# Tap order of a convolution, placement of the first chunks' TensorE work, and order of the loads, in a fused convolution and gated MLP kernel

## Chip, cores, metric

One Trainium2 chip, one core. The metric is device time in microseconds (us). The kernel before took 718.42 us (median of 3 runs, 718.25 to 720.43). "TensorE", "VectorE", "ScalarE", "GpSimd" and "SyncE" are PE, DVE, ACT, POOL and SP in the profile's lines. SBUF and PSUM are the two memories in which the kernel puts its tiles; the matmuls write to PSUM, and to "evict" is to copy a result from there to SBUF. A "tap" is one of the filter's 7 weights, and here also the one VectorE instruction that applies it to one group of channels of one chunk. The "granted clock" is the share of TensorE's full clock that the profile shows, 1.00 at full.

## The reference

```python
# x: (8, 4096, 192); weight: (8 heads, 7 taps); w_in: (192, 2048); w_out: (2048, 192); beta: (2048,)
w = softmax(weight, axis=-1)                      # causal depthwise convolution, one filter per head
x_pad = concatenate([zeros(B, 6, D), x], axis=1)
conv[b, s, h, g] = sum_k w[h, k] * x_pad[b, s + k, h, g]        # 8 heads x 24 channels = 192
h = conv.reshape(B * S, D) @ w_in
g = h * sigmoid(beta * h)
out = g @ w_out
```

## The kernel before

The work goes in steps of 512 tokens of two batch halves (chunk 0 is split in two half steps of 256 tokens, so step 0 and 1 are chunk 0, and step s from 2 on is chunk s-1). The 192 channels lie as three groups of 64; the two halves of the batch fill the 128 partitions. In step s, piece u (16 of them) TensorE makes one hidden block of step s and the share u of the outputs of step s-1. VectorE, meanwhile, convolves the chunk of step s+2, tap by tap, and evicts outputs from PSUM. Chunks from 2 on reach SBUF by a cast to bf16 in DRAM (GpSimd queue) and a transposing DMA (SyncE queue). Chunk 0 and 1 are transposed by TensorE, and chunk 0 is also convolved by TensorE, with diagonal matrices, so that there is something to do early.

The taps, group by group; each of the last six reads what the one before wrote:

```python
    if k == 0:
        nc.vector.tensor_scalar_mul(dst, src, scalar)                          # L330
    else:
        nc.vector.scalar_tensor_tensor(                                        # L332
            out=dst, in0=src, scalar=scalar, in1=dst, op0=ALU.mult, op1=ALU.add)
return [lambda j=j, k=k: tap(j, k) for j in range(NG) for k in range(K)]
```

The eviction of outputs, in VectorE's same queue, which runs in program order (the timeline below shows an eviction wanted from about 45 us on run at 52.82, behind taps written ahead of it; `psum_o` has two buffers, so the outputs two allocations later wait for it):

```python
    nc.vector.tensor_copy(dst, po[:, 0, 0 : 2 * D])                            # L389
    nc.vector.tensor_tensor(dst, po[:, 1, 0 : 2 * D], dst, ALU.add)            # L390
```

The order of work in the first step, and the loop:

```python
extra = {(0, 1): first_xt,                  # TensorE transposes, second half of chunk 0
         (0, 3): lambda: copy_w_in(2),      # VectorE copies of w_in to the other 64 partitions
         (0, 4): first_conv,                # 21 diagonal matmuls, second half of chunk 0
         (0, 6): lambda: copy_w_in(3),
         (0, 8): second_xt}                 # 24 transposes: chunk 1, whose taps can start after this
for s in range(N_ST + 1):
    if s + 2 < N_ST:
        queue.extend(conv_ops(s + 2))
    for u in range(NF):
        if s < N_ST: hidden(s, u)
        if s > 0:    output(s - 1, u)
        if (s, u) in extra: extra[s, u]()
        if s > 0 or u > 8:
            for _ in range(4 if s == 0 else 2 - u % 2):
                if queue: queue.popleft()()
        # [cut] cast(s + 4) at u == 0, transposing DMA of chunk s + 2 at u == 1
```

Ahead of the loop GpSimd scales `w_out` by 1/beta (`prep_w_out`, four instructions) and then issues the casts of chunks 2 and 3.

Of the kernel before, what the change touches and what calls it, by code (L numbers as in the profile page):

```python
# [9 lines left out]
FP32 = mybir.dt.float32  # L10
FP32R = mybir.dt.float32r
BF16 = mybir.dt.bfloat16
# [5 lines left out]
def kernel(  # L18
# [17 lines left out]
    nc = tc.nc  # L36

    B, S, D = x.shape
    H, K = weight.shape
    F = moe_w_in.shape[1]  # L40
    group = D // H
    DG = 64
    NG = D // DG
    TOK = 512
    NF = F // 128
    PAD = K - 1
    HALO = 16
    BLK = 128
# [4 lines left out]
    steps = [(0, 0, TOK // 2), (0, TOK // 2, TOK // 2)]  # L53
# [6 lines left out]
    consts = ctx.enter_context(tc.tile_pool(name="consts", bufs=1))  # L60
    setup = ctx.enter_context(tc.tile_pool(name="setup", bufs=1))
# [4 lines left out]
    ct_pool = ctx.enter_context(tc.tile_pool(name="ct", bufs=3))  # L66
    g_pool = ctx.enter_context(tc.tile_pool(name="g", bufs=2))
    osb_pool = ctx.enter_context(tc.tile_pool(name="osb", bufs=3))
    psum_h = ctx.enter_context(
        tc.tile_pool(name="psum_h", bufs=2, space=bass.MemoryType.PSUM)  # L70
    )
    psum_o = ctx.enter_context(
        tc.tile_pool(name="psum_o", bufs=2, space=bass.MemoryType.PSUM)
    )
# [34 lines left out]
    NB = TOK // BLK  # L109
    HB = NB // 2  # L110
    x0 = setup.tile([128, NB, 2, D], FP32)
    x0b = setup.tile([128, NB, 2, D], BF16)
    x1b = setup.tile([128, NB, 2, D], BF16)

    def load_x(eng, dst, t0, b0, nb):
        for h in range(2):
            eng.dma_start(
                out=dst[:, b0 : b0 + nb, h, :],
                in_=x_v[0, t0 : t0 + nb * BLK, h, :].rearrange(
                    "(b q) d -> q b d", q=BLK  # L120
                ),
            )
# [1 line left out]
    cw8 = setup.tile([H, K], FP32)  # L124
    nc.scalar.dma_start(out=cw8, in_=weight)
    load_x(nc.sync, x0, 0, 0, HB)
    beta_q = setup.tile([NF, 128], FP32)
    nc.sync.dma_start(out=beta_q, in_=moe_beta.rearrange("(c p) -> c p", p=128))
    load_x(nc.sync, x0, HB * BLK, HB, HB)

    zeros = setup.tile([128, TOK], BF16)
# [10 lines left out]
    def load_w_in(i):  # L142
        cols = slice(i * FW, (i + 1) * FW)
        nc.gpsimd.dma_start(  # L144
            out=w_in_s[0:DG, :, cols],
            in_=moe_w_in[:, cols].rearrange("(c d) f -> d c f", c=NG),
        )

    def copy_w_in(i):
        cols = slice(i * FW, (i + 1) * FW)  # L150
        nc.vector.tensor_copy(w_in_s[DG : 2 * DG, :, cols], w_in_s[0:DG, :, cols])  # L151
# [9 lines left out]
        out=sel,  # L161
        in_=sel,
        compare_op=ALU.is_ge,
        fill=0.0,
# [5 lines left out]
        out=sel,  # L170
        in_=sel,
        compare_op=ALU.is_ge,
        fill=0.0,
# [3 lines left out]
    )  # L177
    ident = setup.tile([128, 128], FP32)
    make_identity(nc, ident)
    for i in range(1, NW):  # L180
        load_w_in(i)
    load_x(nc.gpsimd, x1b, TOK, 0, NB)
    w_out_raw = setup.tile([128, NF, D], FP32)
    w_out_v = moe_w_out.rearrange("(c p) d -> p c d", p=128)
    for c in range(0, NF, 4):
        nc.sync.dma_start(out=w_out_raw[:, c : c + 4, :], in_=w_out_v[:, c : c + 4, :])


    nmax = setup.tile([H, 1], FP32)
    nc.vector.reduce_max(nmax, cw8, axis=mybir.AxisListType.X, negate=True)  # L190
    ssum = setup.tile([H, 1], FP32)
    nc.scalar.activation(cw8, cw8, AF.Exp, bias=nmax, accum_out=ssum)
    nc.scalar.activation(warm, warm, AF.Silu)
    rsum = setup.tile([H, 1], FP32)
    nc.vector.reciprocal(rsum, ssum)
    nc.vector.tensor_scalar_mul(cw8, cw8, rsum)
    pc = psum_o.tile([128, 2, TOK], FP32, name="po")

    def fill(n):
        for _ in range(n):  # L200
            nc.tensor.matmul(pc[:, 1, :], zeros[:, 0:128], zeros, start=True, stop=True)  # L201

    fill(5)
    for c in range(NG):
# [4 lines left out]
            start=True,  # L209
            stop=True,  # L210
        )
    nc.tensor.transpose(pc[:, 0, 32 : 32 + NF], beta_q, ident[0:NF, 0:NF])
    fill(3)
    ident_b = setup.tile([128, 128], BF16)
    nc.vector.tensor_copy(ident_b, ident)
    nc.vector.tensor_copy(x0b[:, 0:HB], x0[:, 0:HB])
    cw = consts.tile([128, NG, K], FP32)
    nc.vector.tensor_copy(cw.rearrange("p c k -> p (c k)"), pc[:, 0, 0 : NG * K])
    beta = consts.tile([128, NF], FP32)
    nc.vector.tensor_copy(beta, pc[:, 0, 32 : 32 + NF])  # L220
    beta_r = setup.tile([128, NF], FP32)
    nc.vector.reciprocal(beta_r, beta)


    diag = setup.tile([128, NG, K, 128], FP32R)

    def diag_v(c):
        nc.vector.tensor_tensor(  # L228
            diag[:, c, :, :],
            ident.unsqueeze(1).to_broadcast((128, K, 128)),  # L230
            cw[:, c, :].unsqueeze(2).to_broadcast((128, K, 128)),
            ALU.mult,
        )

    def transposes(xb, b0, nb):
        pt = psum_o.tile([128, NG, nb * BLK], BF16, name="po")
        for b in range(nb):
            for c in range(NG):
                for h in range(2):
                    nc.tensor.transpose(  # L240
                        pt[h * DG : (h + 1) * DG, c, b * BLK : (b + 1) * BLK],
                        xb[:, b0 + b, h, c * DG : (c + 1) * DG],
                        ident_b,
                    )
        return pt

    xt0 = setup.tile([128, NG, HALO + TOK], FP32R)
    nc.vector.memset(xt0[:, :, 0:HALO].bitcast(FP32), 0.0)
    cts = {}

    def diag_conv(s, c, pv):
        n = steps[s][2]
        o = HALO - PAD + steps[s][1]
        for k in range(K):
            nc.tensor.matmul(  # L255
                pv[:, c, :],
                diag[:, c, k, :],
                xt0[:, c, o + k : o + k + n],
                start=(k == 0),
                stop=(k == K - 1),  # L260
            )

    n0 = HB * BLK
    pt = transposes(x0b, 0, HB)
    for k in range(K):
        nc.scalar.mul(diag[:, 0, k, :], ident, cw[:, 0, k : k + 1])  # L266
    diag_v(1)
    nc.scalar.copy(xt0[:, 0:2, HALO : HALO + n0], pt[:, 0:2, :])  # L268
    nc.vector.tensor_copy(xt0[:, 2, HALO : HALO + n0], pt[:, 2, :])
    diag_v(2)  # L270
    copy_w_in(0)
    ct = ct_pool.tile([128, NG, TOK], BF16, name="ct")
    cts[0] = ct
    pv = psum_h.tile([128, 4, n0], FP32, name="ph")
    for c in (1, 0, 2):
        diag_conv(0, c, pv)
        if c == 0:
            nc.scalar.copy(ct[:, c, 0:n0], pv[:, c, :])  # L278
        else:
            nc.vector.tensor_copy(ct[:, c, 0:n0], pv[:, c, :])  # L280
    nc.vector.tensor_copy(x0b[:, HB:NB], x0[:, HB:NB])
    copy_w_in(1)

    def first_xt():

        pt = transposes(x0b, HB, HB)
        nc.vector.tensor_copy(xt0[:, :, HALO + n0 :], pt)

    def first_conv():
        ct = ct_pool.tile([128, NG, TOK], BF16, name="ct")  # L290
        cts[1] = ct
        pv = psum_o.tile([128, 4, n0], FP32, name="po")
        for c in range(NG):
            diag_conv(1, c, pv)
        nc.vector.tensor_copy(ct[:, :, 0:n0], pv[:, 0:NG, :])  # L295

    def second_xt():
        xt = new_xt(1)
        pt = transposes(x1b, 0, NB)
        nc.vector.tensor_copy(xt[:, :, HALO - PAD : HALO], xt0[:, :, HALO + TOK - PAD :])  # L300
        nc.vector.tensor_copy(xt[:, :, HALO:], pt)

    w_out_s = consts.tile([128, NF, D], BF16)

# [14 lines left out]
    def conv_ops(s):  # L319
        ch, t0, n = steps[s]  # L320

        def tap(j, k):
            if j == k == 0:
                cts[s] = ct_pool.tile([128, NG, TOK], BF16, name="ct")
            o = HALO - PAD + k + t0
            src = xts[ch][:, j, o : o + n]
            dst = cts[s][:, j, 0:n]
            scalar = cw[:, j, k : k + 1]
# [4 lines that stand above are left out]
                    out=dst, in0=src, scalar=scalar, in1=dst, op0=ALU.mult, op1=ALU.add  # L333
                )

        return [lambda j=j, k=k: tap(j, k) for j in range(NG) for k in range(K)]

    gs = {}

# [22 lines left out]
    def output(s, u):  # L362
# [33 lines left out]
                )  # L396


    extra = {
        (0, 1): first_xt,  # L400
        (0, 3): lambda: copy_w_in(2),
        (0, 4): first_conv,
        (0, 6): lambda: copy_w_in(3),
        (0, 8): second_xt,
    }
    queue = deque()
    for s in range(N_ST + 1):
        if s + 2 < N_ST:
            queue.extend(conv_ops(s + 2))
        for u in range(NF):  # L410
            if s < N_ST:
                hidden(s, u)
            if s > 0:
                output(s - 1, u)
            if (s, u) in extra:
                extra[s, u]()
            if s > 0 or u > 8:
                for _ in range(4 if s == 0 else 2 - u % 2):
                    if queue:
                        queue.popleft()()  # L420
            if u == 0 and s + 4 < N_CH:
                cast(s + 4)
            if u == 1 and s + 2 < N_CH:
                xpose(s + 2)
# [30 lines left out]
```

## Time and profile before

| | before |
|---|---|
| time, median of 3 | 718.42 us |
| span of the profiled run | 717.5 us |
| TensorE / VectorE / ScalarE busy | 692.2 / 592.2 / 578.5 us |
| one piece (hidden and outputs) in the steady part | 1.308 us, 20.9 us per step |

TensorE is busy nearly all the span. These are the page's lines of busy time and one of its costliest groups, that of the taps (columns of a group: count, then busy time and mean ns of one, then idle time before them):

```profile
span 717.5 us, 24845 instructions
PE 692.2 (96%) x11465; PEld 529.2 (74%) x11465; DVE 592.2 (83%) x935; ACT 578.5 (81%) x543; POOL 67.3 (9%) x79
...
L332 DVE SCALAR_TENSOR_TENSOR ct<-xt,cw,ct 128x512 bf16<-128x512 bf16 x558 | 418.6, 750 | 16.6
```

From 100 to 600 us TensorE is busy 100.00 us in each 100 us, and VectorE 88.1 to 90.4 us, so nothing that VectorE does can matter there: a step costs VectorE less than TensorE's 20.9 us. Only the first 80 us have room. First the table of waits for 30 to 90 us (engine and line that waited, releaser: us in total, times, longest):

```profile
PE po L380 <- DVE osb L390: 10.7, 2, 8.3
```

Those two waits in the timeline of TensorE (start, length, what, count; in brackets the idle time before it and what ended it):

```profile
44.56 1.18 PE L349 MATMUL ph<-ct,w_in_s 64*128 64x512 bf16 x6
54.02 0.82 PE L380 MATMUL po<-w_out_s,g 64*128 64x192 bf16 x8 [8.28 <-DVE osb L390]
...
76.36 0.83 PE L349 MATMUL ph<-ct,w_in_s 64*128 64x512 bf16 x6
79.62 0.83 PE L380 MATMUL po<-w_out_s,g 64*128 64x192 bf16 x16 [2.43 <-DVE osb L390]
```

And why VectorE was late, in its own timeline:

```profile
30.24 0.35 DVE L330 TENSOR_SCALAR ct<-xt,cw 128x512 bf16<-128x512 bf16 x1
30.63 4.69 DVE L332 SCALAR_TENSOR_TENSOR ct<-xt,cw,ct 128x512 bf16<-128x512 bf16 x6
35.23 0.35 DVE L330 TENSOR_SCALAR ct<-xt,cw 128x512 bf16<-128x512 bf16 x1
...
52.82 0.55 DVE L389 COPY osb<-po 128x384 f32<-128x384 f32 x1
53.41 0.56 DVE L390 TENSOR_TENSOR osb<-po,osb 128x384 f32<-128x384 f32 x1
53.88 2.31 DVE L332 SCALAR_TENSOR_TENSOR ct<-xt,cw,ct 128x512 bf16<-128x512 bf16 x3
```

VectorE waits for nothing from 30.24 on. The eviction that TensorE needs from about 45 us on stands behind 32 taps. Two things can be read from the gaps between starts. Six dependent taps take 4.69 us, so they start (4.69 - 0.75) / 5 = 0.788 us apart. The next tap that depends on nothing starts at 35.23, before the end of the record in front of it (30.63 + 4.69 = 35.32): it overlaps by 0.09 us.

Last, the clock. The table of stretches (columns: busy time of each engine with counts, then the granted TensorE clock, DMA share, GB/s) shows that TensorE works at half clock for 3.5 us after the long wait:

```profile
50.70:54.00 3.30, 0.00 (x0) 0.00 (x0) 3.19 (x6) 0.00 (x0) 2.58 (x3) 0.50 2.44 156
54.00:57.50 3.50, 3.48 (x28) 2.21 (x29) 3.40 (x5) 1.11 (x1) 2.30 (x4) 0.52 2.45 156
57.50:60.00 2.50, 2.50 (x42) 1.70 (x38) 2.37 (x4) 2.20 (x3) 1.45 (x2) 1.00 2.05 189
```

### The profile page before, as it was taken

To read this page: it belongs to the slowest core of one execution; us is meant where nothing else is said; L and a number is where in the kernel's file an instruction comes from. 1 tells how busy PE (TensorE), PEld (TensorE's weight loads), DVE (VectorE), ACT (ScalarE), POOL (GpSimd) and SP (SyncE) were. 2 spreads that over 40 slices of the span, in tenths; PEclk is the share of its full clock that TensorE was granted. 3 is DMA by queue.
4 is the path that set the end of the run, shared out by engine and by line. 5 is a ranking of instruction groups with operands and counts; after the bars stand their busy time and mean duration, and the time that the engine had idled before them with its cause. 6 is when DMAs were issued, how large, how long until landed. Compare 5 with 4: busy or idle time off the path is not lost.

```text
span 717.5 us, 24845 instructions
## 1 busy us (share of the span) xinstructions
PE 692.2 (96%) x11465; PEld 529.2 (74%) x11465; DVE 592.2 (83%) x935; ACT 578.5 (81%) x543; POOL 67.3 (9%) x79
## 2 busy tenths in 40 slices
PE   6959899999999999999999999999999999999996
PEld 3646677777777777777777777777777777777776
DVE  3699999898988889898888989888898988887213
ACT  3658788888888888888888888888888888888881
POOL 6765551000000000000000000000000000000000
PEclk9999999999999999999999999999999999999999
DMA  9999999311223221132233112232211322211012
GB/s 198 125 157 166 166 170 172 68 49 44 68 68 52 64 70 49 43 69 68 52 64 69 49 44 68 68 53 62 69 51 42 70 68 53 62 46 46 25 46 68
DMA packets 183113, 54.57 MB, mean 76 GB/s; under 512 B 146384, under 2 KB 183008, under 8 KB 183008
## 3 DMA queue, kind: packets, MB, share of 16 engines
q0 software_dynamic: 97600, 13.31, 27.7%
q1 hardware_dynamic: 85392, 39.67, 23.5%
q8 instruction: 89, 1.46, 0.8%
q14 instruction: 16, 0.13, 0.1%
q10 hardware_dynamic: 16, 0.00, 0.0%
HBM read 28.98 MB, written 37.29 MB: 92 GB/s over the span
## 4 chain that ended last, share of the span: by engine, by line
PE 90%; DVE 7%; ACT 1%; DMA 1%; issue 0%; SPq 0%; DVEq 0%
PE po L380 45%; PE ph L349 43%; DVE ct L332 5%; DMA beta_q<-in_moe_beta_dram 1%; PE ph L255 1%; DVE ct L330 0%; DVE osb L390 0%; PE po L255 0%; DVE osb L389 0%; ACT diag L266 0%; ACT g L356 0%; DVE w_in_s L151 0%; PE po L240 0%; PE po L201 0%; DVE diag L228 0%
## 5 line engine op out<-in xcount | busy, mean ns | idle before, releaser
L356 ACT ACTIVATE g<-ph,beta 128x1024 bf16<-128x1024 f32 (+1 forms) x528 | 572.2, 1088 | 112.9 <-PE ph L349 108.8
L380 PEld LDWEIGHTS <-g 64*128 64x128 bf16 x8192 | 369.9, 94 | 113.8 <-issue 12.5
L380 PE MATMUL po<-w_out_s,g 64*128 64x192 bf16 x8192 | 430.9, 243 | 11.0 <-DVE osb L390 10.7
L332 DVE SCALAR_TENSOR_TENSOR ct<-xt,cw,ct 128x512 bf16<-128x512 bf16 x558 | 418.6, 750 | 16.6
L349 PE MATMUL ph<-ct,w_in_s 64*128 64x512 bf16 (+1 forms) x3168 | 428.7, 372 | 1.9 <-ACT g L356 1.3
L349 PEld LDWEIGHTS <-w_in_s 64*128 64x128 bf16 x3168 | 164.1, 94 | 57.2 <-issue 5.2
L389 DVE COPY osb<-po 128x384 f32<-128x384 f32 x128 | 71.4, 558 | 83.4 <-PE po L380 82.9
L390 DVE TENSOR_TENSOR osb<-po,osb 128x384 f32<-128x384 f32 x128 | 71.3, 557 | 4.4
L95 POOL DMA_DIRECT2D xd<-in_x_dram x60 | 54.9, 918 | 38.0 <-DMA xd<-in_x_dram 35.9
L330 DVE TENSOR_SCALAR ct<-xt,cw 128x512 bf16<-128x512 bf16 x93 | 32.9, 354 | 0.0
L255 PE MATMUL ph<-xt_151,diag 128*128 128x256 f32 x21 | 5.6, 439 | 4.6 <-ACT xt_151 L268 2.2
L255 PEld LDWEIGHTS ph<-xt_151,diag 128*128 128x128 f32 x21 | 4.7, 326 | 5.4 <-ACT xt_151 L268 2.4
L306 POOL TENSOR_TENSOR w_out_s<-w_out_raw,beta_r 128x768 bf16<-128x768 f32 x4 | 5.9, 1468 | 5.3 <-DMA w_out_raw<-in_moe_w_out_dram 3.8
L278 ACT CAST ct<-ph 128x256 bf16<-128x256 f32 x1 | 0.4, 373 | 5.7 <-PE ph L255 5.7
L201 PE MATMUL po<-zeros 128*128 128x512 bf16 x8 | 3.8, 627 | 1.3 <-DVE warm L134 1.3
L266 ACT ACTIVATE diag<-ident,cw 128x128 fp32r<-128x128 f32 x7 | 2.2, 389 | 3.4 <-DVE beta L220 3.4
L151 DVE COPY w_in_s<-w_in_s 64x1536 bf16<-64x1536 bf16 x4 | 4.5, 1135 | 0.1
L280 DVE CAST ct<-ph 128x256 bf16<-128x256 f32 x2 | 0.8, 425 | 4.4 <-PE ph L255 4.3
L295 DVE CAST ct<-po 128x768 bf16<-128x768 f32 x1 | 1.0, 958 | 3.3 <-PE po L255 3.3
L144 POOL DMA_DIRECT2D w_in_s<-in_moe_w_in_dram x4 | 2.9, 735 | 0.8 <-POOLq L439 0.8
L255 PEld LDWEIGHTS po<-xt_151,diag 128*128 128x128 f32 x21 | 2.5, 189 | 0.3 <-issue 0.3
L255 PE MATMUL po<-xt_151,diag 128*128 128x256 f32 x21 | 2.7, 285 | 0.0
(44 smaller groups left out, 24.5 us busy)
## 6 DMA issues: line engine op xcount, KB each, us to landing
out_dram<-osb SPq DMA_DIRECT2D x62, 384.0 KB, 3.0
xd<-in_x_dram POOLq DMA_DIRECT2D x54, 198.0 KB, 13.0
w_out_raw<-in_moe_w_out_dram SPq DMA_DIRECT2D x4, 384.0 KB, 8.2
xd<-in_x_dram POOLq DMA_DIRECT2D x6, 192.0 KB, 14.6
x_83<-in_x_dram SPq DMA_DIRECT2D x4, 192.0 KB, 3.9
w_in_s<-in_moe_w_in_dram POOLq DMA_DIRECT2D x4, 192.0 KB, 7.5
out_dram<-osb SPq DMA_DIRECT2D x4, 192.0 KB, 5.5
xt<-xd SPq DMA_TRANSPOSE x30, 5.3
```

The lines of the kernel that those rows point to most:

```text
L95: nc.gpsimd.dma_start(out=xd[r0:, :, h, :], in_=x_v[p, t0:t1, h, :].rearrange("t (c d) -> t c d", c=NG),)
L151: nc.vector.tensor_copy(w_in_s[DG : 2 * DG, :, cols], w_in_s[0:DG, :, cols])
L201: nc.tensor.matmul(pc[:, 1, :], zeros[:, 0:128], zeros, start=True, stop=True)
L255: nc.tensor.matmul(pv[:, c, :], diag[:, c, k, :], xt0[:, c, o + k : o + k + n], start=(k == 0), stop=(k == K - 1),)
L306: nc.gpsimd.tensor_tensor(w_out_s[:, c0 : c0 + n, :], w_out_raw[:, c0 : c0 + n, :], beta_r[:, c0 : c0 + n].unsqueeze(2).to_broadcast((128, ...
L330: nc.vector.tensor_scalar_mul(dst, src, scalar)
L332: nc.vector.scalar_tensor_tensor(out=dst, in0=src, scalar=scalar, in1=dst, op0=ALU.mult, op1=ALU.add)
L349: nc.tensor.matmul(ph[:, h, 0:n], w_in_s[rows, j, cols], cts[s][rows, j, 0:n], start=(j == 0), stop=(j == NG - 1),)
L356: nc.scalar.activation(gs[s][:, fc, :, 0:n], ph[:, :, 0:n], AF.Silu, scale=beta[:, fc : fc + 1])
L380: nc.tensor.matmul(po[:, r, b * D : (b + 1) * D], g[rows, fc, h, q * BLK : (q + 1) * BLK], w_out_s[rows, fc, :], start=(fc == 0), stop=(fc ...
L389: nc.vector.tensor_copy(dst, po[:, 0, 0 : 2 * D])
L390: nc.vector.tensor_tensor(dst, po[:, 1, 0 : 2 * D], dst, ALU.add)
```

## The change

It has three intents: (1) let consecutive taps belong to different groups, so that none waits for the one before; (2) cut the early TensorE work in small pieces between the hidden blocks, and bring chunk 1's transposes ahead of the second half's convolution, so that its taps can start sooner; (3) load in order of need: chunk 1 before the later pieces of `w_in`, `w_out` last and on GpSimd's queue, beta out of the way of the first small matmuls.

```diff
-        return [lambda j=j, k=k: tap(j, k) for j in range(NG) for k in range(K)]
+        return [lambda j=j, k=k: tap(j, k) for k in range(K) for j in range(NG)]
...
-    beta_q = setup.tile([NF, 128], FP32)
-    nc.sync.dma_start(out=beta_q, in_=...)            # and its transpose ahead of the fills
+    (load from ScalarE's queue; transpose after the second small convolution)
...
+    load_x(nc.gpsimd, x1b, TOK, 0, NB)                # chunk 1
     for i in range(1, NW):
         load_w_in(i)
-    load_x(nc.gpsimd, x1b, TOK, 0, NB)
     for c in range(0, NF, 4):
-        nc.sync.dma_start(out=w_out_raw[:, c : c + 4, :], in_=w_out_v[:, c : c + 4, :])
+        nc.gpsimd.dma_start(out=w_out_raw[:, c : c + 4, :], in_=w_out_v[:, c : c + 4, :])
...
     # [cut] the three small convolutions each get their own PSUM tile;
     # ScalarE's copy of x goes ahead of its seven diagonal builds;
     # the fills, needless matmuls on zeros in the start, go from 8 to 12
...
-    extra = {...}
+    def first_work():
+        first_xt(); copy_w_in(1); yield
+        for _ in second_xt(): yield                   # 6 transposes at a time
+        copy_w_in(2)
+        for i, _ in enumerate(first_conv()):          # up to 3 matmuls at a time
+            if i == 2: copy_w_in(3)
+            yield
...
+            next(work, None)
+            if s > 0: pops = 2 - u % 2
+            else:     pops = 0 if u < 5 else 1 if u < 14 else 6
```

More of the change, by code (lines that the diff above doesn't have):

```diff
@@ L126 @@
     load_x(nc.sync, x0, 0, 0, HB)
-    beta_q = setup.tile([NF, 128], FP32)
-    nc.sync.dma_start(out=beta_q, in_=moe_beta.rearrange("(c p) -> c p", p=128))
     load_x(nc.sync, x0, HB * BLK, HB, HB)
@@ L185 @@
     for c in range(0, NF, 4):
-        nc.sync.dma_start(out=w_out_raw[:, c : c + 4, :], in_=w_out_v[:, c : c + 4, :])
+        nc.gpsimd.dma_start(
+            out=w_out_raw[:, c : c + 4, :], in_=w_out_v[:, c : c + 4, :]
+        )
     nmax = setup.tile([H, 1], FP32)
@@ L192 @@
     nc.scalar.activation(cw8, cw8, AF.Exp, bias=nmax, accum_out=ssum)
+    beta_q = setup.tile([NF, 128], FP32)
+    nc.scalar.dma_start(out=beta_q, in_=moe_beta.rearrange("(c p) -> c p", p=128))
     nc.scalar.activation(warm, warm, AF.Silu)
@@ L211 @@
         )
-    nc.tensor.transpose(pc[:, 0, 32 : 32 + NF], beta_q, ident[0:NF, 0:NF])
-    fill(3)
+    fill(2)
     ident_b = setup.tile([128, 128], BF16)
@@ L218 @@
     nc.vector.tensor_copy(cw.rearrange("p c k -> p (c k)"), pc[:, 0, 0 : NG * K])
-    beta = consts.tile([128, NF], FP32)
-    nc.vector.tensor_copy(beta, pc[:, 0, 32 : 32 + NF])
-    beta_r = setup.tile([128, NF], FP32)
-    nc.vector.reciprocal(beta_r, beta)
     diag = setup.tile([128, NG, K, 128], FP32R)
@@ L233, in diag_v, with transposes @@
         )
-    def transposes(xb, b0, nb):
-        pt = psum_o.tile([128, NG, nb * BLK], BF16, name="po")
+    def transposes(pt, xb, b0, at, nb):
         for b in range(nb):
@@ L240, in transposes @@
                     nc.tensor.transpose(
-                        pt[h * DG : (h + 1) * DG, c, b * BLK : (b + 1) * BLK],
+                        pt[h * DG : (h + 1) * DG, c, (at + b) * BLK : (at + b + 1) * BLK],
                         xb[:, b0 + b, h, c * DG : (c + 1) * DG],
@@ L244, in transposes @@
                     )
-        return pt
     xt0 = setup.tile([128, NG, HALO + TOK], FP32R)
@@ L249, with diag_tap, diag_conv @@
     cts = {}
-    def diag_conv(s, c, pv):
+    def diag_tap(s, c, k, pv):
         n = steps[s][2]
-        o = HALO - PAD + steps[s][1]
-        for k in range(K):
-            nc.tensor.matmul(
-                pv[:, c, :],
-                diag[:, c, k, :],
-                xt0[:, c, o + k : o + k + n],
-                start=(k == 0),
-                stop=(k == K - 1),
-            )
+        o = HALO - PAD + steps[s][1] + k
+        nc.tensor.matmul(
+            pv,
+            diag[:, c, k, :],
+            xt0[:, c, o : o + n],
+            start=(k == 0),
+            stop=(k == K - 1),
+        )
+    def diag_conv(s, c, pv, ct):
+        for k in range(K):
+            diag_tap(s, c, k, pv)
+        if c == 0:
+            nc.scalar.copy(ct[:, c, 0 : steps[s][2]], pv)
+        else:
+            nc.vector.tensor_copy(ct[:, c, 0 : steps[s][2]], pv)
     n0 = HB * BLK
-    pt = transposes(x0b, 0, HB)
-    for k in range(K):
-        nc.scalar.mul(diag[:, 0, k, :], ident, cw[:, 0, k : k + 1])
+    pt = psum_o.tile([128, NG, n0], BF16, name="po")
+    transposes(pt, x0b, 0, 0, HB)
+    fill(3)
     diag_v(1)
@@ L269 @@
     nc.vector.tensor_copy(xt0[:, 2, HALO : HALO + n0], pt[:, 2, :])
+    for k in range(K):
+        nc.scalar.mul(diag[:, 0, k, :], ident, cw[:, 0, k : k + 1])
     diag_v(2)
@@ L273 @@
     cts[0] = ct
-    pv = psum_h.tile([128, 4, n0], FP32, name="ph")
-    for c in (1, 0, 2):
-        diag_conv(0, c, pv)
-        if c == 0:
-            nc.scalar.copy(ct[:, c, 0:n0], pv[:, c, :])
-        else:
-            nc.vector.tensor_copy(ct[:, c, 0:n0], pv[:, c, :])
+    diag_conv(0, 1, psum_h.tile([128, 2, TOK], FP32, name="ph")[:, 0, 0:n0], ct)
+    fill(2)
+    diag_conv(0, 2, psum_h.tile([128, 2, TOK], FP32, name="ph")[:, 0, 0:n0], ct)
+    beta_p = pc[:, 0, 32 : 32 + NF]
+    nc.tensor.transpose(beta_p, beta_q, ident[0:NF, 0:NF])
+    beta = consts.tile([128, NF], FP32)
+    nc.vector.tensor_copy(beta, beta_p)
+    diag_conv(0, 0, psum_o.tile([128, 2, TOK], FP32, name="po")[:, 0, 0:n0], ct)
+    beta_r = setup.tile([128, NF], FP32)
+    nc.vector.reciprocal(beta_r, beta)
     nc.vector.tensor_copy(x0b[:, HB:NB], x0[:, HB:NB])
-    copy_w_in(1)
     def first_xt():
-        pt = transposes(x0b, HB, HB)
+        pt = psum_o.tile([128, NG, n0], BF16, name="po")
+        transposes(pt, x0b, HB, 0, HB)
         nc.vector.tensor_copy(xt0[:, :, HALO + n0 :], pt)
     def first_conv():
-        ct = ct_pool.tile([128, NG, TOK], BF16, name="ct")
-        cts[1] = ct
+        cts[1] = ct_pool.tile([128, NG, TOK], BF16, name="ct")
         pv = psum_o.tile([128, 4, n0], FP32, name="po")
         for c in range(NG):
-            diag_conv(1, c, pv)
-        nc.vector.tensor_copy(ct[:, :, 0:n0], pv[:, 0:NG, :])
+            for k in range(K):
+                diag_tap(1, c, k, pv[:, c, :])
+                if k % 3 == 2 or k == K - 1:
+                    if k == K - 1 and c == NG - 1:
+                        nc.vector.tensor_copy(cts[1][:, :, 0:n0], pv[:, 0:NG, :])
+                    yield
     def second_xt():
         xt = new_xt(1)
-        pt = transposes(x1b, 0, NB)
-        nc.vector.tensor_copy(xt[:, :, HALO - PAD : HALO], xt0[:, :, HALO + TOK - PAD :])
-        nc.vector.tensor_copy(xt[:, :, HALO:], pt)
+        pt = psum_o.tile([128, NG, TOK], BF16, name="po")
+        for b in range(NB):
+            transposes(pt, x1b, b, b, 1)
+            if b == NB - 1:
+                nc.vector.tensor_copy(
+                    xt[:, :, HALO - PAD : HALO], xt0[:, :, HALO + TOK - PAD :]
+                )
+                nc.vector.tensor_copy(xt[:, :, HALO:], pt)
+            yield
     w_out_s = consts.tile([128, NF, D], BF16)
@@ L396, in output @@
                 )
-    extra = {
-        (0, 1): first_xt,
-        (0, 3): lambda: copy_w_in(2),
-        (0, 4): first_conv,
-        (0, 6): lambda: copy_w_in(3),
-        (0, 8): second_xt,
-    }
+    def first_work():
+        first_xt()
+        copy_w_in(1)
+        yield
+        for _ in second_xt():
+            yield
+        copy_w_in(2)
+        for i, _ in enumerate(first_conv()):
+            if i == 2:
+                copy_w_in(3)
+            yield
+    work = first_work()
     queue = deque()
@@ L414 @@
                 output(s - 1, u)
-            if (s, u) in extra:
-                extra[s, u]()
-            if s > 0 or u > 8:
-                for _ in range(4 if s == 0 else 2 - u % 2):
-                    if queue:
-                        queue.popleft()()
+            next(work, None)
+            if s > 0:
+                pops = 2 - u % 2
+            else:
+                pops = 0 if u < 5 else 1 if u < 14 else 6
+            for _ in range(pops):
+                if queue:
+                    queue.popleft()()
             if u == 0 and s + 4 < N_CH:
```

## The prediction

(The 12 us off the kernel before come to 706.)

> **What bounds the kernel now.** TensorE is busy 96% of the 717.5 us span (page, part 1), and in the table of stretches it is busy 100.00 us in every 100 us from 100 to 600. There one piece of hidden work plus its outputs takes 1.308 us (timeline), 20.9 us a step, against 18.9 us of VectorE work. No change to VectorE can be seen there. Only the first 80 us can give.
>
> Those 80 us: the first hidden matmul starts at 18.70; step 0 runs to 33.9; step 1 to 44.56. Then TensorE waits 8.28 us (45.3 to 54.0) and later 2.43 us (77.2 to 79.6), both for VectorE L390 (waits): VectorE runs in order, and its evictions of the outputs stand behind convolution taps. The chain from 30.2 to 79 is almost all L332. The granted clock was 0.66 in 50 to 60: after the wait TensorE ran slow.[...]
>
> **What the change does.**
> 1. *Start.* The transpose of beta waited for its load until 6.17 and held three fills, the copy of the tap weights (7.85) and all behind them. It leaves that place; copy at about 6.4. The copies of x on ScalarE go ahead of seven diagonal builds (2.15 us), and the three small convolutions no longer wait for each other's copies (1.9 us and 0.5 us). Estimate: first hidden matmul at 15.5 instead of 18.7.
> 2. *Step 0.* Blocks of 2.7 us (21 matmuls) and 0.8 us (24 transposes) are spread. ScalarE needs 0.65 us per piece, so 16 take 10.5 us; with waits 11 to 13 instead of 15.2.
> 3. *Taps round the groups.* A dependent tap starts 0.787 us after the one before (750 ns long); where the next instruction does not depend on it, it starts after 0.66 us, overlapping by 0.09.[...] So 21 taps: 14.95 us to about 12.7.
> 4. *Earlier taps.* The second chunk is loaded before the later weights and transposed first, so its taps start at about 21.5 instead of 30.24, but two weight copies and the eviction of the small convolution (1.0 us each) now lie among them: done at about 36 to 37 instead of 45.2.
> 5. *Cost.* w_out comes last on the GpSimd queue, so its scaling ends at about 20 instead of 19.06 and the first cast of x is issued 1 us later; the transposed chunk 2 (about 35 now) lands at 36 to 37, just when VectorE asks for it.
>
> **Sum.** The eviction that ended at 53.97 then ends at about 45; TensorE, there at about 39.5, waits about 5.5 us. Step 3, with its wait, started in effect at 74.4; it would start at 62 to 63, the second wait gone or under 1 us. Minus 12.
>
> **Predicted: 706 us, 8 in 10 between 702 and 712.** Faster by over 2% (under 704.05): 0.27; within 2%: 0.71; slower: 0.02.
>
> **What would show it.** First hidden matmul at 15 to 16; second tap of another group 0.66 us behind the first; taps' group mean about unchanged in record but 21 in under 13.2 us; one wait of 4 to 7 us near 40, the one near 77 under 1 us; 1.308 us per piece afterwards.
>
> **What would make it wrong.** Casts and transpose landing later (w_out late): the eviction stays near 50, time about 711. Taps not overlapping: 2 to 4 us lost. No wait near 40 at all: about 700. The low clock falling away gives 1 us more.

## The result, and the profile after

The changed kernel took 709.81 us (median of 4 runs, 709.44 to 710.24), the kernel before 718.65 us (4 runs, 718.25 to 720.43). The ratio is 0.9872, 95% interval 0.9855 to 0.9890. A ratio here is the mean time of one kernel's runs over that of the other's of the same rounds, so it isn't quite the ratio of the medians.

The same lines of the page after (the taps are line 349 now, and the hidden and output matmuls 366 and 397):

```profile
span 708.0 us, 24854 instructions
PE 694.0 (98%) x11469; PEld 528.7 (75%) x11469; DVE 551.9 (78%) x935; ACT 579.1 (82%) x543; POOL 70.0 (10%) x83
...
L349 DVE SCALAR_TENSOR_TENSOR ct<-xt,cw,ct 128x512 bf16<-128x512 bf16 x558 | 379.0, 744 | 0.0
```

The mean of one tap is 744 ns after 750, which looks like nothing. But the busy time of the same 558 instructions fell from 418.6 to 379.0 us, while their records add up to 558 x 0.744 = 415 us: they overlap now, and busy time counts an overlap once. The mean length of a record doesn't say how fast a queue moves; the distance of the starts does.

The waits of TensorE, 20 to 90 us, and where they fall in its timeline:

```profile
PE po L397 <- DVE osb L407: 5.2, 1, 5.2
PE ph L366 <- DVE ct L305: 1.5, 1, 1.5
```

```profile
25.44 1.04 PE L366 MATMUL ph<-ct,w_in_s 64*128 64x256 bf16 x12
27.97 0.71 PE L366 MATMUL ph<-ct,w_in_s 64*128 64x256 bf16 x6 [1.49 <-DVE ct L305]
...
40.16 0.81 PE L366 MATMUL ph<-ct,w_in_s 64*128 64x512 bf16 x6
46.16 0.82 PE L397 MATMUL po<-w_out_s,g 64*128 64x192 bf16 x8 [5.18 <-DVE osb L407]
```

The long wait is 5.18 us instead of 8.28 and ends 7.86 us sooner; the second (2.43 us) is gone; a small new one, 1.49 us, stands before step 1. VectorE's timeline:

```profile
18.33 1.61 DVE L149 COPY w_in_s<-w_in_s 64x1536 bf16<-64x1536 bf16 x1
19.97 2.65 DVE L347 TENSOR_SCALAR ct<-xt,cw 128x512 bf16<-128x512 bf16 x2
22.66 0.69 DVE L149 COPY w_in_s<-w_in_s 64x1536 bf16<-64x1536 bf16 x1
...
27.82 8.70 DVE L349 SCALAR_TENSOR_TENSOR ct<-xt,cw,ct 128x512 bf16<-128x512 bf16 x13
38.87 0.88 DVE L347 TENSOR_SCALAR ct<-xt,cw 128x512 bf16<-128x512 bf16 x3 [2.35 <-ACT g L373]
39.66 5.38 DVE L349 SCALAR_TENSOR_TENSOR ct<-xt,cw,ct 128x512 bf16<-128x512 bf16 x8
...
45.55 0.56 DVE L407 TENSOR_TENSOR osb<-po,osb 128x384 f32<-128x384 f32 x1
```

Independent taps now start (8.70 - 0.74) / 12 = 0.663 us apart. Taps of chunk 1 begin at 19.97 instead of 30.24 and end at 36.5 instead of 45.3. But then VectorE is idle for 2.35 us. The line names ScalarE, but a wait for several events is put down to one of them, and these taps read nothing that line 373 writes. In the profiles of a_oldtaps, a_gated, a_blocks and a_wout_sp the same wait is put down to the transposing DMA. The chain that ended last shows it here too, by start, length and what:

```profile
7.87 8.49 DMA w_out_raw<-in_moe_w_out_dram
...
16.50 5.97 POOL w_out_s L323 x4
22.48 1.14 POOL xd L95
23.61 5.14 DMA xd<-in_x_dram
...
28.84 9.91 DMA xt<-xd
...
38.87 0.88 DVE ct L347 x3
```

Chunk 2 lands at 38.75, 0.12 us before the tap. It hangs on a queue: the load of `w_out` lands at 16.4, GpSimd scales it until 22.5, and only then, at 22.48, does the same queue issue the cast, whose result the transposing DMA takes. Last, the clock again, in stretches cut where it changes (half clock twice):

```profile
24.70:28.10 3.40, 1.88 (x24) 1.03 (x25) 3.40 (x6) 2.19 (x4) 3.40 (x4) 1.00 2.20 141
28.10:31.50 3.40, 3.40 (x40) 2.88 (x38) 3.40 (x6) 1.60 (x3) 3.40 (x5) 0.51 2.24 143
...
45.20:52.00 6.80, 5.84 (x44) 3.53 (x45) 6.76 (x12) 2.23 (x2) 4.52 (x5) 0.50 2.30 169
```

The milestones, in us from the start of the span:

| | before | predicted | after |
|---|---|---|---|
| first hidden matmul | 18.70 | 15.5 | 13.45 |
| step 0's first outputs (its hidden work done) | 33.88 | 26.5 to 28.5 | 28.46 |
| taps of chunk 1 start | 30.24 | 21.5 | 19.97 |
| taps of chunk 1 end | 45.3 | 36 to 37 | 36.5 |
| chunk 2 has landed | about 35 | 36 to 37 | 38.75 |
| first eviction of step 0's outputs ends | 53.97 | 45 | 46.11 |
| TensorE's wait for it | 8.28 | about 5.5 | 5.18 |
| step 2's first outputs, with a wait that follows | 71.78 + 2.43 | 62 to 63 | 65.08 |

The last row, in which step 2's outputs are made during step 3, differs by 74.21 - 65.08 = 9.1 us, of the 9.5 us between the spans. The steady part is the same: 1.308 us a piece in both.

### The profile page after: what moved, and what is told of

The parts are those of the page before. It is cut to its first block, busy times and chain, and to the rows that moved or that the text cites. A ratio compares the mean times of both kernels' runs of the same rounds, so it can differ in the third digit from the quotient of the medians. Undisturbed runs are those within 1.5% of the kernel's fastest.

```text
span 708.0 us, 24854 instructions
## 1 busy us (share of the span) xinstructions
PE 694.0 (98%) x11469; PEld 528.7 (75%) x11469; DVE 551.9 (78%) x935; ACT 579.1 (82%) x543; POOL 70.0 (10%) x83
## 4 chain that ended last, share of the span: by engine, by line
PE 93%; DMA 3%; POOL 2%; DVE 1%; issue 0%; POOLq 0%; DVEq 0%; SPq 0%
PE po L397 47%; PE ph L366 46%; DMA xt<-xd 1%; DMA w_out_raw<-in_moe_w_out_dram 1%; POOL w_out_s L323 1%; DVE ct L349 1%; DMA xd<-in_x_dram 1%; POOL w_in_s L142 0%; POOL x1b L117 0%; POOL xd L95 0%; DVE osb L407 0%; DVE osb L406 0%; DVE ct L347 0%; POOL sel L158 0%; POOL sel L167 0%
## 5 line engine op out<-in xcount | busy, mean ns | idle before, releaser
L349 DVE SCALAR_TENSOR_TENSOR ct<-xt,cw,ct 128x512 bf16<-128x512 bf16 x558 | 379.0, 744 | 0.0
L366 PEld LDWEIGHTS <-w_in_s 64*128 64x128 bf16 x3168 | 162.2, 94 | 56.4 <-DVE ct L305 1.8
L347 DVE TENSOR_SCALAR ct<-xt,cw 128x512 bf16<-128x512 bf16 x93 | 30.2, 379 | 2.4 <-ACT g L373 2.3
L203 PE MATMUL po<-zeros 128*128 128x512 bf16 x12 | 5.9, 629 | 1.3 <-DVE warm L132 1.3
L249 PE MATMUL po<-xt_145,diag 128*128 128x256 f32 x28 | 6.0, 318 | 0.0
L249 PEld LDWEIGHTS ph<-xt_145,diag 128*128 128x128 f32 x14 | 3.1, 292 | 0.7 <-ACT xt_145 L270 0.3
L249 PE MATMUL ph<-xt_145,diag 128*128 128x256 f32 x14 | 3.6, 419 | 0.0
L184 POOL DMA_DIRECT2D w_out_raw<-in_moe_w_out_dram x4 | 3.1, 775 | 0.0
```

Source lines behind the costliest of these rows:

```text
L203: nc.tensor.matmul(pc[:, 1, :], zeros[:, 0:128], zeros, start=True, stop=True)
L249: nc.tensor.matmul(pv, diag[:, c, k, :], xt0[:, c, o : o + n], start=(k == 0), stop=(k == K - 1),)
L349: nc.vector.scalar_tensor_tensor(out=dst, in0=src, scalar=scalar, in1=dst, op0=ALU.mult, op1=ALU.add)
L366: nc.tensor.matmul(ph[:, h, 0:n], w_in_s[rows, j, cols], cts[s][rows, j, 0:n], start=(j == 0), stop=(j == NG - 1),)
```

## The experiments

Theories: **1**, the first 80 us are set by VectorE's queue, and the tap order shortens that queue. **2**, in the changed kernel the late arrival of chunk 2 (loads and scaling of `w_out` in front of its cast) is what holds VectorE. **3**, the half clock after the wait is a cost by itself. **4** came up on the way: GpSimd's scalings and VectorE's copies and first taps get in each other's way. Rivals stand in the expectations. "b_" is an edit of the kernel before, "a_" of the changed one.

| run | median us (lowest to highest, runs) | ratio to before [95%] |
|---|---|---|
| changed kernel | 709.81 (709.44 to 710.24, 4) | 0.9872 [0.9855, 0.9890] |
| b_taps | 713.31 (712.13 to 714.89, 6) | 0.9919 [0.9904, 0.9933] |
| a_oldtaps | 713.90 (713.01 to 715.12, 6) | 0.9926 [0.9914, 0.9938] |
| a_castfirst | 707.13 (705.69 to 713.64, 6) | 0.9850 [0.9818, 0.9883] |
| a_warm | 708.80 (707.73 to 708.99, 5) | 0.9852 [0.9838, 0.9866] |
| a_gated | 710.08 (709.23 to 710.49, 4) | 0.9878 [0.9865, 0.9892] |
| a_blocks | 709.79 (708.66 to 711.03, 4) | 0.9876 [0.9861, 0.9891] |
| a_actscale | 705.12 (704.73 to 705.65, 5) | 0.9810 [0.9797, 0.9824] |
| a_dupdma | 723.22 (722.43 to 725.07, 5) | 1.0066 [1.0052, 1.0080] |
| a_lock | 707.92 (706.16 to 711.73, 5) | 0.9858 [0.9833, 0.9883] |
| a_wout_sp | 708.68 (706.43 to 709.28, 4) | 0.9851 [0.9833, 0.9870] |
| a_tune | 703.96 (703.34 to 704.28, 4) | 0.9790 [0.9777, 0.9804] |
| a_betaback | 709.08 (708.16 to 710.73, 5) | 0.9851 [0.9830, 0.9872] |

The runs were made in groups, and each group's kernel before had a median of 718.59 to 720.08 us. All gave correct results. Kernels of different groups are compared by their ratios.

### b_taps: only the tap order

```diff
 (kernel before)
-        ... for j in range(NG) for k in range(K)]
+        ... for k in range(K) for j in range(NG)]
```

> The kernel before with one part of the change: the taps go round the three groups, nothing else. Theory 1 (the first 80 us are set by VectorE's queue, and a tap that doesn't depend on the one before starts 0.66 us after it instead of 0.787): taps of one chunk take 12.7 us instead of 14.95, the eviction that ended at 53.97 ends at about 50.4, the wait of TensorE shrinks from 8.3 to about 5 us, the second wait (2.43 us near 77) is gone: 718.6 to about 713, ratio 0.992. Rival (the gain of the change comes from the earlier start and the spread TensorE work, and tap order is only tidier): ratio 0.998 to 1.000.

Measured: 713.31 us, 0.9919. In its profile the eviction ends at 50.78, TensorE's wait is 4.8 us, and the second wait is gone. Theory 1 holds, to the size, and the rival falls: the tap order alone is worth 0.8%.

### a_oldtaps: all but the tap order

```diff
 (changed kernel)
-        ... for k in range(K) for j in range(NG)]
+        ... for j in range(NG) for k in range(K)]
```

> The changed kernel with the taps in the old order (group by group). Theory 1: 11 taps before the first eviction of step 0's outputs cost 1.6 us more, the second wait of TensorE comes back with 1 to 2 us: about 3 us longer than the changed kernel, 712.5 to 713, ratio to the kernel before 0.9915. Part of the 2.2 us per chunk hides in the wait of 2.35 us for the transposed chunk 2. Rival: no difference from the changed kernel, 0.987.

Measured: 713.90 us, 0.9926, a bit more than expected. The waits of TensorE for the evictions sum up to 7.7 us, in two, one of 6.3 us. VectorE's wait for chunk 2 shrinks to 0.94 us, because its taps end later. So the part without the tap order is worth 0.74%, the tap order alone 0.81%, and together they give 1.28%, not 1.55%. The difference of 0.27 points is about as large as its uncertainty; that each eats some of the wait that the other would remove fits the two waits above, but isn't shown by the times.

### a_castfirst: casts ahead of the scaling

```diff
+    cast(2)
+    cast(3)
     for c in range(0, NF, 4):
         prep_w_out(c, 4)
-    cast(2)
-    cast(3)
```

> The changed kernel with the casts of chunks 2 and 3 issued before the scaling of w_out on GpSimd, not after it. Theory 2 (in the changed kernel the chain w_out landing, scaling on GpSimd until 22.4, cast, transpose lands at 38.8 and holds VectorE 2.35 us, and through it TensorE): chunk 2 lands before 36.4, VectorE doesn't wait for it, the eviction ends at about 43.7, TensorE's wait is 2.5 to 3.5 us, perhaps too short for the clock to fall: about 3.5 us shorter than the changed kernel, 706, ratio to before 0.9825; if the clock falls all the same, 2 us shorter. Rival (VectorE's amount of work alone sets it; the record names ScalarE for the 2.35 us): within 0.5 us of the changed kernel.

Measured: 705.69, 705.99, 706.50 and 707.77 us in four runs, 711.50 and 713.64 in the two others. Over all six the ratio is 0.9850, and its interval overlaps that of the changed kernel. The expected 706 is there, and so is something that was not expected. The profiled run is the longest, and its lines of GpSimd and of VectorE show why:

```profile
17.47 5.74 POOL L323 TENSOR_TENSOR w_out_s<-w_out_raw,beta_r 128x768 bf16<-128x768 f32 x4
```

```profile
18.49 5.27 DVE L149 COPY w_in_s<-w_in_s 64x1536 bf16<-64x1536 bf16 x1
```

A copy that takes 0.69 us elsewhere took 5.27 us, and ended 0.55 us after the last of four scalings on GpSimd. TensorE needed that copy, waited 3.44 us to 23.82, and then ran slow until about 31.9 (six hidden matmuls took 0.82 us, before the wait and after 31.9 about 0.5). Chunk 2 was no longer waited for, even in this run. So theory 2 is supported by the four shorter runs, and theory 4 is put up for the two longer ones. It is support only: the split was made after the times were known, and no profile of a shorter run was kept.

The trace shows how long the copy was held: it started at 18.49, in the first scaling, and didn't get in when that one ended at 18.95 (they take 1.48 us each) but only after all four. In the changed kernel the same collision is there, weaker: the copy of 1.61 us at 18.33 and the two first taps that took 2.65 us together at 19.97 (0.35 us each elsewhere) stand beside the scalings from 16.50 to 22.47, of which one took 1.64 us (1.47 in the kernel before).

### a_warm: needless matmuls in the wait

```diff
             if s < N_ST:
                 hidden(s, u)
+            if (s, u) == (2, 0):
+                keep_warm(2, 1, 22)    # 22 matmuls on zeros into the PSUM tile of hidden(2, 1)
             if s > 0:
                 output(s - 1, u)
```

> The changed kernel with 22 needless matmuls on zeros (about 4.75 us) put where TensorE waits near 41 to 46 us, into a PSUM tile that the real work then overwrites. Theory 3 (the half clock from 45.2 to 52.0, which follows the idle wait, is worth 2.9 us): clock stays full, step 2 after the wait takes 16.4 us instead of 18.9; VectorE's next evictions then bind and give back about 1.3 us, so 1 to 2.5 us shorter than the changed kernel, ratio to before 0.9845. Rival (the low clock does not cost time, as ScalarE's 1.02 us per piece binds there): no change, or longer by up to 0.5 us.

Measured: 708.80 us, 0.9852 against 0.9872. In the profile the wait that is left is 2.54 us, and TensorE is back at full pace 3.4 us after its end (49.82 - 46.44) instead of 6.1 us (52.28 - 46.16); three of the five runs had a mean clock of 0.999 or 1.000, against 0.992 for the changed kernel's profiled run. The gain is about 0.2%, or 1.4 us if one takes the ratios at their centres, and the two intervals overlap, so the times alone don't show it. The two profiles do show it: from the wait's end (46.44) to step 2's first outputs (64.00) it took 17.6 us, against 18.9 us in the changed kernel (46.16 to 65.08). So theory 3 is supported, at the low end of what was expected; the clock doesn't account for all of the 3.8 us between the predicted 706 us and the measured time.

### a_gated: fewer casts in flight

```diff
             if u == 0 and s + 4 < N_CH:
+                if s > 0:
+                    nc.gpsimd.tensor_copy(gate, cts[s][:, NG - 1, 0:1])
                 cast(s + 4)
```

> The changed kernel, where every cast from chunk 5 on waits (a one-element copy on GpSimd that reads the convolved chunk of the step) until VectorE has got that far; the order of GpSimd's early work is left as it is. Theory 2 (the late arrival of chunk 2 holds VectorE): the casts no longer fill the DMA queues, the transpose of chunk 2 takes 5 to 6 us from issue to landing instead of 9.9, lands at about 34.5, VectorE's wait of 2.35 us is gone, the eviction ends near 43.7: 706 to 707.5, ratio to before 0.983. Rival A (VectorE's amount of work alone sets it): 0.987 as the changed kernel. Rival B (the transpose takes 10 us whatever else the queues do): 0.987 and the landing unchanged.

Measured: 710.08 us, 0.9878. It was no test. The transpose of chunk 2 took 10.6 us to land (9.9 in the changed kernel), and VectorE waited 3.2 us. But the DMA share from 32 to 36 us was 2.07, against 1.94: the casts of chunks 3 and 4, issued before the first gate at 28.6, kept the queues as full as ever until 44 us (2.19 from 40 to 44, then 0.21). So this run leaves open whether the casts make the transposes slow. Three other profiles say something about it. In a_castfirst and a_lock GpSimd issued no casts while its scalings ran (17.47 to 23.21 and 17.62 to 23.74); the traffic sank to 17 GB/s near 24 us in the one and to 49 GB/s near 24.5 us in the other, and chunk 2's transpose, issued at 23.07 and 23.39, landed after 5.5 and 5.2 us. In a_actscale GpSimd went on issuing casts, the traffic from 22 to 25 us never sank below 147 GB/s, and the transpose issued at 23.85 took 9.2 us. That fits the casts as the cause; no run was made to test it.

### a_blocks: the small pieces undone

```diff
-        for _ in second_xt(): yield
+        for _ in second_xt(): pass           # all after piece 1
...
-        for i, _ in enumerate(first_conv()): ...
+        for _ in first_conv(): pass          # all 21 matmuls after piece 5
```

> The changed kernel with the TensorE work of the first chunks in blocks again (all transposes of chunk 1 after piece 1, all 21 matmuls of the second half's convolution after piece 5), nothing else. Theory 1 (VectorE's queue and the arrival of chunk 2 set the first 80 us; TensorE waits for them anyway): step 0 gets 1 to 2 us longer on TensorE, but this goes into its later wait: within 1 us of the changed kernel, ratio 0.987 plus or minus 0.0015. Rival (the small pieces are what brought the gain in step 0): 2 us or more longer, ratio 0.990 or more.

Measured: 709.79 us, 0.9876: no difference. The cause was not quite the one expected. TensorE came to the wait sooner with blocks, not later, since the small convolution's eviction, no longer behind taps, freed step 1 sooner: it stood idle 9.8 us up to 48.4. What it gained there it lost in that wait, because chunk 2 was waited for until 41.1. Small pieces or blocks: with this queue behind them, neither matters.

### a_actscale: the scaling on ScalarE

```diff
-    for c in range(0, NF, 4):
-        prep_w_out(c, 4)               # GpSimd
     cast(2)
     cast(3)
...
+            if s == 0 and 6 <= u < 14:          # ScalarE, two small products per piece
+                prep_w_out_act(2 * (u - 6))
+                prep_w_out_act(2 * (u - 6) + 1)
```

> Casts of chunks 2 and 3 early as in the run before, and the scaling of w_out on ScalarE (16 small products, two per piece in pieces 6 to 13 of step 0) instead of GpSimd. Theory 4 (in the profiled run with the early casts the VectorE copy of w_in took 5.27 us, as long as GpSimd's four scalings lasted; the two engines shut each other out[...]): no VectorE copy or first tap over 1.2 us before 30, first eviction at 41 to 43, runs within 2 us of each other, 703 to 706, ratio 0.980. ScalarE pays about 5.6 us in step 0, of which about 2 are free. Rival (the spread comes from the DMA queues, or the copy waited for its load): a copy of over 2 us stays, spread of 5 us or more stays.

Measured: 705.12 us, 0.9810, five runs within 0.92 us. The copies took 0.69 to 0.92 us, the two first taps 1.04 us together, VectorE didn't wait for chunk 2, the eviction ended at 42.76, and the mean clock of the profiled run was 0.999 (0.992 in the changed kernel's). TensorE's wait is 1.13 us, and one of 1.30 us follows in step 3. It cost ScalarE 16 products in 8 pairs of about 0.8 us, and pieces of 1.26 us for as long as they lasted. The gain over the changed kernel is clear of the noise. VectorE's lines, for comparison with a_lock below:

```profile
17.71 0.92 DVE L149 COPY w_in_s<-w_in_s 64x1536 bf16<-64x1536 bf16 x1
18.66 1.04 DVE L348 TENSOR_SCALAR ct<-xt,cw 128x512 bf16<-128x512 bf16 x2
19.73 0.69 DVE L149 COPY w_in_s<-w_in_s 64x1536 bf16<-64x1536 bf16 x1
```

Theories 2 and 4 both say this, so it doesn't tell them apart; the next run but one does.

### a_dupdma: copies by DMA

```diff
     def copy_w_in(i):
+        if i > 0:
+            nc.sync.dma_start(out=w_in_s[DG : 2 * DG, :, cols], in_=w_in_s[0:DG, :, cols])
+            return
         nc.vector.tensor_copy(w_in_s[DG : 2 * DG, :, cols], w_in_s[0:DG, :, cols])
```

(Together with the early casts of a_castfirst.)

> Casts of chunks 2 and 3 early, scaling on GpSimd as in the changed kernel, but pieces 1 to 3 of w_in are duplicated to the other partitions by transfers on SyncE's queue instead of VectorE copies. Theory 4: with no copies to be shut out, VectorE's taps start by 19 to 20 (a first tap may still be shut out by the scalings, up to 1.5 us each), first eviction at 42 to 43.5, 704 to 707, runs within 3 us; if the transfers land after the piece that needs them, TensorE waits in step 0 for them. Rival (the copies are cheap, 0.7 to 1 us, and only happened to stand there): no better than the early casts alone, spread of 5 us or more stays.

Measured: 723.22 us, slower than the kernel before. TensorE waited twice for the transfers, 5.3 and 5.9 us. The first took 8.5 us to land. The others stood in SyncE's queue behind the first transposing DMA, which was waiting for its cast until 24.3, so they were issued at 26.46. This is a fault of the experiment's placement: behind a transfer that itself waited, SyncE's queue was no place for a small urgent one. It says nothing about theory 4.

### a_lock: GpSimd's work put back, for nobody

```diff
 (a_actscale)
     cast(2)
     cast(3)
+    for c in range(0, NF, 4):
+        nc.gpsimd.tensor_tensor(unused[:, c : c + 4, :], ...the same operands..., ALU.mult)
```

> The kernel with the scaling of w_out on ScalarE, and GpSimd doing its four scalings all the same, into a tile that nothing reads. Theory 4 (GpSimd's scalings and VectorE's copies and first taps shut each other out): copies or first taps of 1.2 to 5 us come back between 17 and 23, the half clock comes back in some runs, median 1 to 4 us longer than without the needless scalings, runs spread over 3 us or more. Rival (what helped was to have the scaling and with it the first outputs on another engine, not the absence of GpSimd's work): 705 plus or minus 0.7, copies of 0.7 to 0.9 us.

Measured: 707.92 us, 706.16 to 711.73: 0.9858 against 0.9810, so 0.5% longer and 5.6 us wide instead of 0.9 (four of the five runs lie within 2.1 us). Its profiled run is the shortest, and even there VectorE's lines are long beside GpSimd's, and the eviction ends at 43.83 instead of 42.76:

```profile
17.62 6.12 POOL L337 TENSOR_TENSOR unused<-w_out_raw,beta_r 128x768 bf16<-128x768 f32 x4
```

```profile
18.16 2.65 DVE L356 TENSOR_SCALAR ct<-xt,cw 128x512 bf16<-128x512 bf16 x2
20.84 1.84 DVE L149 COPY w_in_s<-w_in_s 64x1536 bf16<-64x1536 bf16 x1
22.71 1.18 DVE L356 TENSOR_SCALAR ct<-xt,cw 128x512 bf16<-128x512 bf16 x1
```

Nothing reads what GpSimd computes here. It also holds back GpSimd's next casts (issued again from 23.69 on), which would be a rival, but from 28 to 90 us VectorE waits for no chunk in either profile. Theory 4 is shown: the collision costs time, 0.5% here. That it makes the time uncertain as well rests on few runs. That the two longer runs of a_castfirst have the same cause as its profiled one is inferred, from their low clock (0.990 and 0.987, where the four others have 0.996).

### a_wout_sp: w_out back on SyncE's queue

```diff
-        nc.gpsimd.dma_start(out=w_out_raw[:, c : c + 4, :], ...)
+        nc.sync.dma_start(out=w_out_raw[:, c : c + 4, :], ...)
```

> The changed kernel with the loads of w_out back on SyncE's queue, nothing else: undoes the last part of the order of need. Theory 2 (w_out at the end of GpSimd's queue is what makes scaling, casts and chunk 2 late): scaling ends near 19 instead of 22.4, chunk 2 lands near 36, VectorE's wait for it is under 1 us, and the scalings are over before most of the copies: 706 to 708.5, unless chunk 1 or the later w_in pieces now land after TensorE asks for them (14.8 for chunk 1). Rival (the order of need is what brought the early start): first taps 2 us or more later, 711 or more.

Measured: 708.68 us, 0.9851. Scaling ends at 19.92, VectorE waits 1.45 us for chunk 2 (expected: under 1), TensorE waits 0.69 us for chunk 1, which lands 9.2 us after its issue instead of 5.6. The time is no longer than the changed kernel's; the intervals overlap, so a gain isn't shown. The rival falls: putting `w_out` last on GpSimd's queue, one of the parts of the change, brought no time.

### a_tune: three taps earlier

```diff
 (a_actscale)
-                pops = 0 if u < 5 else 1 if u < 14 else 6
+                pops = 0 if u < 5 else 1 if u < 11 else 2 if u < 14 else 6
```

> Scaling of w_out on ScalarE, casts early, and three more taps put ahead of the eviction of the small convolution, where VectorE stood idle 1.9 us. If VectorE's queue is what is left: eviction ends near 41, TensorE's waits of 1.1 us (41.7) and 1.3 us (64.4) shrink to under 1 us in sum, 703 to 704, ratio 0.978 to 0.979. Rival (ScalarE's 1.26 us per piece in step 0 now sets it): 705 as before.

Measured: 703.96 us, 0.9790. VectorE's idle 1.93 us before the small convolution's eviction is down to 0.85. The wait near 41.7 is gone, and the one in step 3 is 1.2 us. This is the shortest of all kernels here: 2.1% under the kernel before, 0.8% under the changed one (0.9790 / 0.9872). Its interval touches that of a_actscale, so the gain from the three taps alone is barely clear of the noise.

### a_betaback: one step of the faster start undone

```diff
+    nc.tensor.transpose(pc[:, 0, 32 : 32 + NF], beta_q, ident[0:NF, 0:NF])
     fill(2)
...
-    nc.tensor.transpose(beta_p, beta_q, ident[0:NF, 0:NF])
```

> The changed kernel with the transpose of beta put back ahead of the fills and the copy of the tap weights (its load is still issued from ScalarE's queue): undoes the first step of the faster start alone. The first hidden matmul comes 1.5 to 2 us later (near 15). Theory 2 (in the changed kernel the arrival of chunk 2 at 38.8, which hangs on the loads of w_out and GpSimd, sets what follows, and VectorE has 2.35 us to spare before it): VectorE's taps of chunk 1 end near 38.2, still before chunk 2, and the time is within 0.6 us of the changed kernel, 709.5 to 710.5, ratio 0.987 to 0.988. Rival (the start is on the critical path all along): 1.5 to 2 us longer, 711.5, ratio 0.9895 or more.

Measured: 709.08 us, 0.9851. TensorE waits 1.91 us for beta, the tap weights are copied at 8.48 instead of 6.30, and the first hidden matmul comes at 14.52 instead of 13.45. VectorE's taps of chunk 1 end at 37.05, still before chunk 2 at about 39.2. No time is lost; the ratio even came out a little under the expected 0.987 to 0.988. The rival falls, for as much as was undone: 1.07 us of a later start cost nothing. This agrees with theory 2, which gives VectorE 2.35 us to spare before chunk 2, but it doesn't test by itself what makes chunk 2 late.

## Why the prediction was right, and where its sizes were off

The measured 709.81 us lies within 702 to 712, and "within 2%" was the likeliest class. The mechanism was right: VectorE's queue, seen through one late eviction. The size was not: it said 12 us; the spans of the two profiled runs differ by 9.5 us and the medians by 8.8.

1. *What bounds it.* Right. The steady part didn't move at 1.308 us a piece, and 9.1 of the 9.5 us are gained before step 2's first outputs.
2. *"First hidden matmul at 15.5."* It came at 13.45. The first copy of `w_in` took 0.78 us instead of the 1.84 us it had before, when it stood beside a scaling on GpSimd (12.06 to 13.53); the third small convolution took 1.09 us instead of 1.86. How much this helped isn't known: a_betaback gave back 1.07 us of it and lost no time.
3. *"With waits 11 to 13 instead of 15.2"* for step 0. Wrong: it took 28.46 - 13.45 = 15.0 us. The estimate took ScalarE's 0.65 us as the pace of a piece, but in TensorE's timeline a piece with three diagonal matmuls takes 0.99 us (hidden work starts at 18.21 and again at 19.20) and one with a single one 0.75 us (19.20 to 19.95), and the 1.49 us of waiting for the small convolution's eviction, queued behind six taps, were not foreseen. That step 0 was done at 28.46, within the predicted 26.5 to 28.5, is luck: a start 2 us sooner and a step at least 2 us longer cancelled. a_blocks, with blocks in place of pieces, took the same time in the end.
4. *Taps, "14.95 us to about 12.7".* Right: 0.26 us for each of the three first and 0.66 us for each of the 18 others is 12.7. b_taps measures its worth alone: 0.8%.
5. *Taps start 21.5, done 36 to 37.* Started at 19.97, ended at 36.5; the lead of 1.5 us was lost to the collision with GpSimd (a copy of 1.61 us and two first taps of 2.65 us), so that the end came out as said is luck too.
6. *"Its scaling ends at about 20 instead of 19.06 ... lands at 36 to 37."* This is the term that was mis-sized. Scaling ended at 22.47, because the loads of `w_out`, last in GpSimd's queue, landed only from 16.4 on, and the four scalings were still to come. Chunk 2 landed at 38.75, and VectorE, ready at 36.5, waited 2.35 us. a_castfirst, a_wout_sp and a_betaback agree with it, none of them as a clear difference in time. The prediction had named this risk (*"w_out late"*, with "time about 711"), and the measured 709.81 lies nearer to that than to its 706.
7. *The sum.* The eviction ended 1.1 us later than said. From the wait's end to step 2's first outputs it took 65.08 - 46.16 = 18.9 us; the prediction's numbers allow 17.5. Most of that is the clock: the half clock covered 5.84 us of TensorE's work after the wait, before only 3.48, because the wait ended sooner after the clock fell (0.96 us after 45.20; before, 3.3 us after 50.70). At half rate (from a hidden block's start to that of the next outputs it took 1.28 us, 0.65 afterwards) that is (5.84 - 3.48) / 2 = 1.2 us, an estimate; a_warm, back at full pace 3.4 us after its wait instead of 6.1, took 17.6 us for the same stretch. The prediction had treated it as a bonus (*"the low clock falling away gives 1 us more"*); it was a loss instead.

What stays open: whether it is the casts that make a transposing DMA slow (chunk 2's took 9.9 us from issue to landing, the median of the changed kernel's 30 is 4.9, and a_lock had 5.2 at about the same place; see a_gated), what makes the clock fall, what the lateness of chunk 2 costs by itself, and which part of the change other than the tap order brought its 0.74% (a_oldtaps). Chunk 1's earlier load and earlier transposes, which let its taps start 10 us sooner, are the likely part, but no run undid them alone. For `w_out`'s place in the queue, the small pieces and 1.07 us of the start, undoing them cost no time that shows. As to the clock: it fell in the waits of 8.28 and 5.18 us and stayed at 1.00 in the one of 2.43 us (77.20 to 79.60), but it also fell at 28.10 in the changed kernel, after 3.40 us with 1.88 us of TensorE work and no wait over 1.5 us, while in the kernel before 3.40 us with 1.48 us of work (12.60 to 16.00) kept the full clock. The runs don't show what sets it.

## What to carry to other kernels

Work back from the wait that ends last to the queue it comes from, and ask of each part of a change whether it shortens that queue: here the tap order did, and the small pieces and a microsecond of the start didn't. A queue that both computes and issues DMAs made what stood behind it wait here (GpSimd, scaling `w_out` until 22.47, issued the cast at 22.48, and chunk 2 held VectorE for 2.35 us); issue first, compute later, and on an engine whose work doesn't lengthen a busy neighbour's (beside GpSimd's scalings copies of 0.69 us took 1.61 and 5.27, with the scaling on ScalarE 0.69 to 0.92). Interleave independent chains in an engine's queue, and judge that by the distance of starts (0.788 to 0.663 us here), not by the length of the records (750 to 744 ns).
